# Last stage of a mixer: wo loaded through two queues, a gated tile in a free staging slot, transposes behind attention

## The chip, the cores and the metric

The kernel runs on one core of one Trainium2 chip. The metric is the device time of one execution in microseconds (us), the median of the runs; lower is better.

## What is computed

Two branches work on the same normalized input and are added to it. Branch A is linear attention with a softmax feature map, branch B a gated MLP whose gate mixes all 2048 tokens. All is float32.

```python
# S = 2048 tokens, D = 512, H = 32 heads of 16, Fh = 688
xn  = layernorm(x)
q, k, v = split_heads(xn @ wqkv)
phi(t)  = concat(softmax(t @ w_phi), softmax(-t @ w_phi))     # 32 features a head
kv  = phi(k)^T v ;  z = sum_s phi(k)
o   = phi(q) kv / (phi(q) z + 1e-6)
A   = o @ wo
zz  = gelu(xn @ w_in) ; z1 = zz[:, :Fh] ; z2 = layernorm(zz[:, Fh:])
B   = (z1 * (w_sp @ z2 + b_sp)) @ w_out
out = x + A + B
```

## The kernel before

The tokens lie in 16 tiles of 128 (`NT`), handled in pairs. A float32 product is made of three fp32r matmuls over a high part `h` and a rest `l` (`mm3`, lines L51 to L53): ScalarE rounds the high part (`round_h`, L43), VectorE subtracts to get the rest (`rest_l`, L47). The stages are: projections of the input and the sum `kv`; the second half of the MLP's input (`z2`, split into operands `B`); the token-mixing product in a seven-product block form (names P1 to P7, tile `g`); and the last stage, which this change touches.

In the seven-product stage a block of two row tiles takes four passes (`products`), `drain` adds the seven PSUM banks into `c` and `gate` multiplies by the gelu of `z1` and stores the gated tile to DRAM as `u_d`. The last block is drained when the last stage begins. Its passes also free the 16 slots of the pool `xz`, one after the other, as the operands `B` are used up; function `slot` gives such a slot to a tile of the last stage: six for `w_out` (`wu`), one each for `zb`, `u_uh`, `ul_rt`, `et`, `qtmp`, two for the first two feature tiles (`eq`), one for `et` of tile 3, one for `c`. One more slot comes free in the same pass and is not used until later.

The last stage computes, for each pair of tiles i and i+1:

- `attend_T`: 16 TensorE transposes of the features (`ptq`, L749 or L751), copied to `f` by ScalarE (L753); `attend`: the products with `kvT` (`po`, L765; sixteen in the program, which the profile counts as thirty-two), rounded and split into `oT` by ScalarE and VectorE.
- `gated`, that is `gate_T`: six transposes of a gated tile `u` (`ptu`, four on L640, then L644 and L645), split into `uh`, `ul` and `rt`.
- `project_u`: seventeen matmuls of `uh`, `ul`, `rt` with `wu` into `pout`; `project_o`: twelve matmuls of `oT` with `wo` into the same bank; then VectorE adds `x` (`xr`, L788) and SyncE stores the result.
- `features`: VectorE scales the features of a later tile (`q_fin`, L380 to L387), GpSimd's queue copies them to `er`.

Entering it, PE does in this order: the last `g` matmuls, the transposes of gated tile 1, `project_u(0)`, `attend_T(0)`, `project_u(1)`, `attend`, the transposes of gated tiles 2 and 3, `project_o(0)` and `project_o(1)`. The wo matrix is loaded in four chunks (`load_w`, `wof`), each by four transfers of 32 rows; ScalarE rounds a chunk to `woh`, VectorE makes `wol`.

A scheduler orders the instructions of each engine when the kernel is built; `tc.issue_after(ins)` only puts what stands inside it behind `ins` in that order. The waits come from the data and from reused memory. The queues are served in order: SyncE's (SP in the profile) carries nearly all loads of this stage, GpSimd's (POOL) the `er` copies and `z1t`. GpSimd's transfers are software queue q0 of the page, SyncE's are in hardware queue q1.

The lines that load wo and fetch gated tile 1:

```python
us[1] = fetch_u(1)                       # a tile of pool cw, opened when the last pass's memory is given back
...
load_w(wo, rows, wo_h[:, c], wo_l[:, c], cw.tile([P, D], F32, tag="wof", bufs=4, name="wof"))
```

Of the kernel before, what the change touches and what calls it, by code (L numbers as in the profile page):

```python
# [10 lines left out]
F32 = mybir.dt.float32  # L11
F32R = mybir.dt.float32r
# [6 lines left out]
P = 128  # L19
S, D, H, DH, FH = 2048, 512, 32, 16, 688  # L20
# [6 lines left out]
REM = FH - KF * P  # L27
# [8 lines left out]
def mixer(ctx: ExitStack, tc: tile.TileContext, x, x_t, wv, wqkT, phi_bd, wo, w_in, wst, b_r, w_out, out):  # L36
    nc = tc.nc
    pe, act, dve, pool, sp = nc.tensor, nc.scalar, nc.vector, nc.gpsimd, nc.sync


    def round_h(eng, h, src):
        if eng is act:
            return act.activation(h, src, AF.Copy).ins  # L43
        return eng.tensor_copy(h, src).ins

    def rest_l(l, src, h, eng=None):
        return (eng or dve).tensor_tensor(l, src, h.bitcast(F32), op=ALU.subtract).ins  # L47
# [113 lines left out]
    with ExitStack() as p0:  # L161
# [32 lines left out]
        def fold(wT, g, accs):  # L194
            gs = slice(g * P, (g + 1) * P)
            for c, acc in accs:
                ins = pe.matmul(acc[:, gs], wT[g][:, c * P:(c + 1) * P], bd[:, gs], start=g == 0, stop=g == NG - 1,
                                skip_group_check=True).ins
            return ins
# [26 lines left out]
        def split_x(src):  # L226
            t = xz.tile([P, 2, FH], F32R, tag="xz", name="xT")
            xT.append(t)
            src = src.rearrange("p a b -> p (a b)")
            return round_h(act, t[:, 0, :D], src), rest_l(t[:, 1, :D], src, t[:, 0, :D])  # L230

        def stats(s):
            st6 = wk.tile([P, 6], F32, tag="st6", name="st6")
            dve.bn_stats(st6, xt[s])
            nm = wk.tile([P, 1], F32, tag="nm", name="nm")
            ins = dve.bn_aggr(mv_x[:, s], st6).ins
            pool.tensor_scalar_mul(nm, mv_x[:, s, 0:1], -1.0)
            rstd_of(mv_x[:, s], r_x[:, s:s + 1])
            return nm, ins
# [4 lines left out]
        def transposed(s):  # L244
            xs = xt.pop(s)
            pt = ps.tile([P, ND, P], F32, tag="mm", name="pt")
            for c in range(ND):
                ins = pe.transpose(pt[:, c], xs[:, c * P:(c + 1) * P], ident).ins  # L248
            return pt, ins
# [46 lines left out]
        with ExitStack() as queue:  # L296
# [3 lines left out]
            nm, i = stats(0)  # L300
            keep(dve=i, act=center(0, nm))
            accs = [(c, (za, kv_ps_p)[c // 2].tile([P, D], F32, tag="z", name="fold")) for c in range(ND)]
            for g in range(NG):
                if g == NG - 1:
                    pt, i = transposed(0)
                    keep(pe=i)
                keep(pe=fold(wkT, g, accs))
            i, j = split_x(pt)
            keep(act=i, dve=j)
            nm, i = stats(1)  # L310
# [10 lines left out]
            pt, i = transposed(1)  # L321
            keep(pe=i)
            i, j = split_x(pt)
            keep(act=i, dve=j)
            nm, i = stats(2)
# [3 lines left out]
            for k in range(2):  # L329
                accs = [(2 * k + m, za.tile([P, D], F32, tag="z", name="fold")) for m in range(2)]  # L330
                for g in range(NG):
                    i = fold(wqT, g, accs)
                folded(0, accs)
                if k == 0:
                    keep(pe=i)
                    pt, i = transposed(2)
# [63 lines left out]
    def load_a(n):  # L400
        i, q = SEQ[n]
        f = []
        for k in range(2):
            t = ws.tile([P, QC, P], F32, tag=f"f{k}", bufs=2, name="wf")
            sp.dma_start(t, wst[2 * i + k, :, q * QC:(q + 1) * QC, :])
            f.append(t.rearrange("p (k two) t -> p two k t", two=2))
        return f
# [167 lines left out]
    def load_z1(i):  # L575
        t = gt.tile([P, 2, FH + REM], F32, tag="z1", name="z1t")
        for k in range(2):
            pool.dma_start(t[:, k, :FH], z1_d[2 * i + k])
        return t

    def products(n, g):
        i, q = SEQ[n]
        ops = A.pop(n)
        for name, an, bn in FORM:
            if n % NQ == 0:
                g[name] = psg.tile([P, D], F32, tag="g", name="g")
            dst = g[name][:, :FC]
            for k in range(2):
                (ah, al), (bh, bl) = ops[an], B[2 * q + k][bn]
                mm3(dst, (ah[:, k], al[:, k]), (bh, bl), n % NQ == 0 and k == 0, n % NQ == NQ - 1 and k == 1)  # L590
# [32 lines left out]
    def slot(name, dt=F32):  # L623
        return xz.tile([P, 2, FH], dt, tag="xz", name=name).rearrange("p a b -> p (a b)")

    def load_w(src, parts, h, l, t):
        rows = 0
        for r0, r1 in parts:
            sp.dma_start(t[rows:rows + r1 - r0], src[r0:r1, :])
            rows += r1 - r0  # L630
        return round_h(act, h, t[:rows]), rest_l(l, t[:rows], h)

    def load_u(i, t):
        sp.dma_start(t.bitcast(F32), u_d[i])
        return t
# [18 lines left out]
    def first_gate(i):  # L654
        a, b = slot("u_uh", F32R), slot("ul_rt", F32R)
        u = load_u(i, a[:, :FH + REM])
        return gate_T(psg, "g", u, k_tiles(a[:, FH + REM:]), k_tiles(b[:, :KF * P]), b[:2 * REM, KF * P:(KF + 1) * P])

    lasts, wu = [None] * 5, []

    def first_q(s):
        e = slot("eq", F32R)[:, :NF]
        sp.dma_start(e.bitcast(F32), e_d[s, :, :NF])
        return e

    def stage_w():
        t = [xz2.tile([P, 2, 2, FC], F32, tag="b", name="wof").rearrange("p a b c -> p (a b c)") for _ in range(3)]
        w = [slot("wu", F32R) for _ in range(KF + 1)]
        for c in range(KF + 1):
            n = P if c < KF else 2 * REM  # L670
            h, l = (w[c][:n, k * D:(k + 1) * D] for k in range(2))
            rows = [(c * P, (c + 1) * P)] if c < KF else [(KF * P, FH)] * 2
            load_w(w_out, rows, h, l, t[c // 2][:, c % 2 * D:(c % 2 + 1) * D])
            wu.append((h, l))

    g, es, ets = {}, {}, {}
    for n in range(NC):
        i = SEQ[n][0]
        if n % NQ == 1 and i < NP - 1:
            z = load_z1(i)  # L680
        products(n, g)
        if n % NQ == NQ - 1 and i < NP - 1:
            gate(i, drain(i, g, gt.tile([P, 4, FC], F32, tag="c", name="c")), z)
            g = {}
        if n + 3 < NC:
            raw[n + 3] = load_a(n + 3)
        if n + 2 < NC:
            A[n + 2] = prep_a(n + 2, raw.pop(n + 2))
        if n == NC - 4:
            stage_w()  # L690
        if n == NC - 3:
            zs = slot("zb", F32R)
            zb, ident_r = zs[:, :NF].bitcast(F32), zs[:, NF:NF + P]
            round_h(act, ident_r, ident)
            sp.dma_start(zb, zb_d)
            uT = [first_gate(0)]
            ets[2] = load_q(2, slot("et"))
            es[2], last = q_fin(ets.pop(2), slot("qtmp")[:, :NF], zb)
        if n == NC - 2:
            es[0], es[1] = first_q(0), first_q(1)  # L700
            ets[3] = load_q(3, slot("et"))
    cb = drain(NP - 1, g, slot("c").rearrange("p (a b) -> p a b", a=4))
# [4 lines left out]
    gt = p2.enter_context(right("gl", 1))  # L707
    cw = ctx.enter_context(left("cw", 1))
    wk = ctx.enter_context(left("cwk", 2))
    us, fin = {}, []  # L710

    def fetch_u(i):
        return load_u(i, cw.tile([P, FH + REM], F32R, tag="u", bufs=4, name="u"))
# [11 lines left out]
    def gated(z, ps=None):  # L725
        return gate_T(*(ps or (pst, "tr")), z, wk.tile([P, KF, P], F32R, tag="uh", name="uh"),
                      wk.tile([P, KF, P], F32R, tag="ul", name="ul"), wk.tile([2 * REM, P], F32R, tag="rt", name="rt"))

    us[1] = fetch_u(1)
    kvT = cw.tile([P, 2 * NG, QP], F32, name="kvT")  # L730
    with tc.issue_after(cb[1]), tc.issue_after(cb[2]):
        uT.append(gated(us.pop(1), (psg, "g")))
# [60 lines left out]
    wo_h, wo_l = (cw.tile([P, ND, D], F32R, name=f"wo{k}") for k in "hl")  # L793
    p = {0: project_u(0, uT.pop(0))}
    with tc.issue_after(lasts[0]), tc.issue_after(lasts[1]), tc.issue_after(fin[-1]):
        for c in range(ND):
            rows = [(r, r + QP) for r in range((c % 2 * NG * 2 + c // 2) * QP, D, 2 * QP)][:NG]
            load_w(wo, rows, wo_h[:, c], wo_l[:, c], cw.tile([P, D], F32, tag="wof", bufs=4, name="wof"))
    fT = attend_T(0)
    p[1] = project_u(1, uT.pop(0))  # L800
    oT, ins = attend(fT)
# [13 lines left out]
    nxt = {}  # L815
    for i in range(0, NT, 2):
        if i:
            p[i] = project_u(i, nxt.pop(i))
            if i + 2 < NT:
                nxt[i + 2] = gated(us.pop(i + 2))  # L820
            with tc.issue_after(lasts[2]):
                oT, _ = attend(fT)
            with tc.issue_after(lasts[3]):
                p[i + 1] = project_u(i + 1, nxt.pop(i + 1))
        else:
            nxt[2] = gated(us.pop(2))
        if i + 3 < NT:
            nxt[i + 3] = gated(us.pop(i + 3))
        for k in range(2):
            project_o(i + k, oT, p.pop(i + k))  # L830
            ahead(i + k)
        if i == GATE_LAST:
            with tc.issue_after(lasts[0]), tc.issue_after(lasts[1]):
                gate(NP - 1, cb, z)
            p2.close()
        if i + 2 < NT:
            with tc.issue_after(lasts[4]):
                fT = attend_T(i + 2)
# [33 lines left out]
```

## Time and profile before

| | us |
|---|---|
| runs | 648.68, 649.03, 650.23 |
| median of the runs | 649.03 |
| the profiled execution, its own time | 649.57 |
| its span in the profile | 647.8 |
| TensorE (PE) busy in it | 638.2 |
| VectorE (DVE) busy | 509.5 |
| ScalarE (ACT) busy | 278.7 |
| GpSimd (POOL) busy | 96.3 |

The span is the first to the last recorded instruction; the profiled execution took 1.8 us beside it. Times in rows of the trace count from the start of the span. The granted TensorE clock is full throughout (the page's row of tenths shows 9, which means 90% or more; the windows of the last stage show 1.00 or 0.99). Two of the three runs lie below the profiled execution.

A row of the timeline reads: start, duration, engine, line, operation, output and inputs, shape, count, and in brackets how long the engine sat idle before it and what ended that. Matmuls overlap in the pipeline, so the time that one takes away from the next is the distance of the starts, not the duration.

### The profile page before, as it was taken

Reading aid. Unit: us, or ns where it says so; the run is one execution under the profiler, and the core shown is the slowest. Engines: PE = TensorE matmul, PEld = TensorE weight load, DVE = VectorE, ACT = ScalarE, POOL = GpSimd, SP = SyncE. Lnnn points to the kernel's source line nnn. Section 1 sums busy time; section 2 is a strip of 40 time slices with the busy share of each in tenths; the row PEclk is TensorE's granted clock in tenths of the full one; section 3 lists DMA queues with packets and bytes.
Section 4 is the critical chain, followed back from the end, with each engine's and each line's share of the span. In section 5 each row is a group of like instructions: output and inputs, shape, how many; then the busy total and the mean of one; then the engine's idle time right before and its main releaser. Section 6 shows DMA issues by size and latency. Waiting matters only on the chain.

```text
span 647.8 us, 11206 instructions
## 1 busy us (share of the span) xinstructions
PE 638.2 (99%) x4291; PEld 576.1 (89%) x4291; DVE 509.5 (79%) x922; ACT 278.7 (43%) x464; POOL 96.3 (15%) x185
## 2 busy tenths in 40 slices
PE   7999999999999999999999999999999899999997
PEld 6888888888888999999999999999999677888885
DVE  4988888898889579889978778678696498989521
ACT  5644344332333437887443434434353332323330
POOL 3332221101100104542010010110100000001000
PEclk9999999999999999999999999999999999999999
DMA  8265345533463951002453352544548677775620
GB/s 308 76 165 129 110 119 121 155 114 102 125 183 98 291 187 66 2 2 65 142 179 124 122 175 79 172 128 120 178 157 277 201 271 261 243 264 222 225 66 32
DMA packets 39077, 98.12 MB, mean 151 GB/s; under 512 B 4880, under 2 KB 7184, under 8 KB 39024
## 3 DMA queue, kind: packets, MB, share of 16 engines
q1 hardware_dynamic: 27824, 56.51, 27.4%
q0 software_dynamic: 8896, 35.26, 18.0%
q10 hardware_dynamic: 2304, 5.64, 2.3%
q8 instruction: 33, 0.54, 0.3%
q14 instruction: 20, 0.16, 0.1%
HBM read 56.24 MB, written 26.48 MB: 128 GB/s over the span
## 4 chain that ended last, share of the span: by engine, by line
PE 95%; DMA 2%; DVE 1%; SPq 1%; ACT 0%; issue 0%; POOL 0%; ACTq 0%; POOLq 0%
PE g L53 11%; PE g L52 11%; PE g L51 11%; PE proj L53 7%; PE proj L51 7%; PE proj L52 7%; PE zps L53 6%; PE zps L52 6%; PE zps L51 6%; PE pout L51 5%; PE pout L53 5%; PE pout L52 5%; PE po L765 2%; PE kvps L273 1%; PE ptq L751 1%; PE pt L248 1%
## 5 line engine op out<-in xcount | busy, mean ns | idle before, releaser
L53 PE MATMUL g<-B,A 128*128 128x344 f32 x448 | 143.3, 320 | 0.0
L52 PE MATMUL g<-B,A 128*128 128x344 f32 x448 | 143.2, 320 | 0.0
L51 PE MATMUL g<-B,A 128*128 128x344 f32 x448 | 143.2, 320 | 0.0
L53 PEld LDWEIGHTS g<-B,A 128*128 128x128 f32 x448 | 84.2, 188 | 0.0
L51 PEld LDWEIGHTS g<-B,A 128*128 128x128 f32 x448 | 84.2, 188 | 0.0
L52 PEld LDWEIGHTS g<-B,A 128*128 128x128 f32 x448 | 84.1, 188 | 0.0
L47 DVE TENSOR_TENSOR A<-S,A 128x512 fp32r<-128x512 f32 x64 | 43.8, 690 | 33.6 <-ACT A L43 32.7
L43 ACT ACTIVATE A<-S 128x512 fp32r<-128x512 f32 x64 | 40.1, 631 | 58.9 <-PE g L53 36.0
L110 ACT ACTIVATE e<-e,r_x 128x1024 f32<-128x1024 f32 x32 | 36.8, 1151 | 41.2 <-DVE e L109 40.4
L51 PE MATMUL proj<-wqk_h,xT 128*128 128x512 f32 x128 | 51.4, 401 | 0.3 <-ACT wqk_h L43 0.3
L52 PE MATMUL proj<-wqk_l,xT 128*128 128x512 f32 x128 | 50.5, 394 | 1.1 <-DVE wqk_l L47 1.1
L43 ACT ACTIVATE A<-wf 128x512 fp32r<-128x512 f32 x64 | 33.4, 522 | 40.6 <-PE g L53 39.7
L53 PE MATMUL proj<-wqk_h,xT 128*128 128x512 f32 x128 | 50.9, 397 | 0.0
L51 PE MATMUL zps<-w_0h,xT 128*128 128x344 f32 x128 | 41.8, 326 | 0.0
L112 DVE TENSOR_REDUCE sm<-e 128x64 f32<-128x1024 f32 x32 | 38.7, 1208 | 3.3 <-ACT e L110 3.3
L51 PE MATMUL zps<-w_1h,xT 128*128 128x344 f32 x128 | 41.0, 320 | 0.0
L53 PE MATMUL zps<-w_0h,xT 128*128 128x344 f32 x128 | 41.0, 321 | 0.0
L53 PE MATMUL zps<-w_1h,xT 128*128 128x344 f32 x128 | 41.0, 320 | 0.0
L52 PE MATMUL zps<-w_0l,xT 128*128 128x344 f32 x128 | 40.9, 320 | 0.0
L52 PE MATMUL zps<-w_1l,xT 128*128 128x344 f32 x128 | 40.9, 319 | 0.0
L47 DVE TENSOR_TENSOR A<-wf,A 128x512 fp32r<-128x512 f32 x64 | 35.5, 555 | 3.4 <-ACT A L43 3.0
L753 ACT ACTIVATE f<-ptq 128x512 f32<-128x512 f32 x32 | 16.5, 602 | 33.6 <-PE ptq L751 27.1
(194 smaller groups left out, 1429.2 us busy)
## 6 DMA issues: line engine op xcount, KB each, us to landing
wf<-in_wst SPq DMA_DIRECT2D x64, 256.0 KB, 3.3
e_d<-e POOLq DMA_DIRECT2D x16, 544.0 KB, 5.0
et<-e_d SPq DMA_DIRECT2D x16, 544.0 KB, 5.2
zacc<-e POOLq DMA_DIRECT2D x16, 512.0 KB, 5.3
er<-et POOLq DMA_DIRECT2D x12, 512.0 KB, 4.1
u_d<-z1t POOLq DMA_DIRECT2D x16, 368.0 KB, 4.1
u<-u_d SPq DMA_DIRECT2D x15, 368.0 KB, 4.6
z_d<-z1f ACTq DMA_DIRECT2D x16, 344.0 KB, 3.4
```

Of the source, the lines that this page charges most:

```text
L43: return act.activation(h, src, AF.Copy).ins
L47: return (eng or dve).tensor_tensor(l, src, h.bitcast(F32), op=ALU.subtract).ins
L51: pe.matmul(dst, ah, bh, start=start, stop=False)
L52: pe.matmul(dst, ah, bl, start=False, stop=False)
L53: return pe.matmul(dst, al, bh, start=False, stop=stop).ins
L110: act.activation(e, e, AF.Exp, scale=scale)
L112: dve.tensor_reduce(sm, heads(e), axis=AX.X, op=ALU.add)
L248: ins = pe.transpose(pt[:, c], xs[:, c * P:(c + 1) * P], ident).ins
L273: pe.matmul(kv_acc[k:k + QP, m // 4], vs[:, m * QP:(m + 1) * QP], e[:, m * HP:(m + 1) * HP], start=s == 0 and m < 4, stop=s == NT - 1, ski ...
L751: pe.transpose(pt[:, a, k].bitcast(F32R), src, ident_r)
L753: act.activation(f, pt.rearrange("p a k b -> p a (k b)"), AF.Copy)
L765: lasts[3] = pe.matmul(po[r][c * QP:(c + 1) * QP, j // NG], kvT[rows, j], fs[j // 2][rows, j % 2], start=True, stop=True).ins
```

## The change

Three edits in the last stage. First, `load_w` gets the queue as an argument; wo's chunks 0 and 2 are loaded by SyncE, chunks 1 and 3 by GpSimd. Second, gated tile 1 is fetched into the free slot of `xz`, ahead of the loads of the first features, instead of into a tile of pool `cw`. Third, the transposes of the second gated tile of a pair come behind that pair's attention products in the order.

```diff
-    def load_w(src, parts, h, l, t):
+    def load_w(queue, src, parts, h, l, t):
         rows = 0
         for r0, r1 in parts:
-            sp.dma_start(t[rows:rows + r1 - r0], src[r0:r1, :])
+            queue.dma_start(t[rows:rows + r1 - r0], src[r0:r1, :])
...
-            load_w(w_out, rows, h, l, t[c // 2][:, c % 2 * D:(c % 2 + 1) * D])
+            load_w(sp, w_out, rows, h, l, t[c // 2][:, c % 2 * D:(c % 2 + 1) * D])
...
         if n == NC - 2:
+            us = {1: load_u(1, slot("u1", F32R)[:, :FH + REM])}
             es[0], es[1] = first_q(0), first_q(1)
...
-    us, fin = {}, []
+    fin = []
...
-    us[1] = fetch_u(1)
...
-            load_w(wo, rows, wo_h[:, c], wo_l[:, c], cw.tile([P, D], F32, tag="wof", bufs=4, name="wof"))
+            load_w((sp, pool)[c % 2], wo, rows, wo_h[:, c], wo_l[:, c], cw.tile([P, D], F32, tag="wof", bufs=4, name="wof"))
...
         if i + 3 < NT:
-            nxt[i + 3] = gated(us.pop(i + 3))
+            with tc.issue_after(lasts[3]):
+                nxt[i + 3] = gated(us.pop(i + 3))
```

The number of matmuls, of ScalarE and VectorE operations and of bytes moved stays the same. How the order changes is seen at three places.

On SyncE's queue, at the passage from the seven-product stage to the last one, the pieces of the two programs differ as follows (- before, + now; `u_5390` is gated tile 1 in its new slot, `eq` the first features, `wof` the rows of wo):

```order
 L634 DMA u_uh<-u_d 128x736
 L373 DMA et<-e_d 128x1088
+L634 DMA u_5390<-u_d 128x736
 L663 DMA eq<-e_d 128x1024 x2
 L373 DMA et<-e_d 128x1088
-L634 DMA u<-u_d 128x736
 L735 DMA kvT<-kvT_d 128x256
-L629 DMA wof<-in_wo 32x512 x16
+L629 DMA wof<-in_wo 32x512 x8
 L634 DMA u<-u_d 128x736 x2
```

Gated tile 1 moves ahead of three loads of features, which each come one place later, and eight of wo's sixteen transfers leave the queue.

On GpSimd's queue at the same passage:

```order
 L619 DMA u_d<-z1t 128x736 x2
 L578 DMA z1t<-z_d 128x688 x2
-L723 DMA er<-et 128x1024 x10
+L629 DMA wof<-in_wo 32x512 x8
+L724 DMA er<-et 128x1024 x10
 L619 DMA u_d<-z1t 128x736 x2
```

The eight transfers come behind the last load of `z1t` and ahead of all copies of features.

On ScalarE at the same passage (`c<-g` is the drain's first step, which copies P1's bank; `ptu_5332` is the second bank of gated tile 0's transposes):

```order
-L597 ACTIVATE c<-g 128x344
 L43 ACTIVATE u_uh<-ptu_5332 128x128
+L597 ACTIVATE c<-g 128x344
 L648 ACTIVATE ul_rt<-ptu_5332 96x128
 L43 ACTIVATE uh<-ptu 128x512
 L43 ACTIVATE uh<-ptu_5475 128x128
 L648 ACTIVATE rt<-ptu_5475 96x128
-L43 ACTIVATE woh<-wof 128x512 x4
-L753 ACTIVATE f<-ptq 128x512 x4
+L43 ACTIVATE woh<-wof 128x512 x3
+L753 ACTIVATE f<-ptq 128x512 x4
+L43 ACTIVATE woh<-wof 128x512
```

The drain's first step now stands behind a rounding of gated tile 0, and the last chunk of wo behind the four copies to `f`.

On PE, in the pair i = 2 of the last stage, before (the block left out is the rest of `project_u`):

```order
L645 MATMUL ptu_5760<-zb,u 96x128
L765 MATMUL po<-f,kvT 32x256 x12
L640 MATMUL ptu<-zb,u 128x128 x4
L765 MATMUL po<-f,kvT 32x256 x4
L51 MATMUL pout<-wu,uh 128x512
...
L779 MATMUL pout<-wu,rt 128x512 x2
L644 MATMUL ptu_5818<-zb,u 128x128
L645 MATMUL ptu_5818<-zb,u 96x128
```

and now:

```order
L645 MATMUL ptu_5760<-zb,u 96x128
L765 MATMUL po<-f,kvT 32x256 x16
L51 MATMUL pout<-wu,uh 128x512
...
L779 MATMUL pout<-wu,rt 128x512 x2
L640 MATMUL ptu<-zb,u 128x128 x4
L644 MATMUL ptu_5818<-zb,u 128x128
L645 MATMUL ptu_5818<-zb,u 96x128
```

The four transposes that cut the attention products of pair i = 2 in two now stand behind `project_u`; in pair i = 4 the same is moved, and from pair 6 on PE's order is as it was, since there the transposes already stood behind.

## The prediction

> **What bounds the kernel now.** I read the page first, then PE's list of waits, then PE's timeline through the last stage, and last the timelines of the engines and queues that PE waits for there.
>
> ```profile
> PE 638.2 (99%) x4291; PEld 576.1 (89%) x4291; DVE 509.5 (79%) x922; ACT 278.7 (43%) x464; POOL 96.3 (15%) x185
> ...
> PE 95%; DMA 2%; DVE 1%; SPq 1%; ACT 0%; issue 0%; POOL 0%; ACTq 0%; POOLq 0%
> ```
>
> PE is busy nearly always, and 95% of the chain that ended last is PE's own work. So time is saved only where PE waits, or where its order costs extra. The list of PE's waits from 480 us on has two lines (total, times, longest):
>
> ```profile
> PE ptu L640 <- DMA u<-u_d: 1.3, 1, 1.3
> PE po L765 <- ACT f L753: 0.7, 1, 0.7
> ```
>
> Both are where the last stage begins. PE's timeline there, one row for each change of work:
>
> ```profile
> 503.08 0.32 PE L53 MATMUL g<-B,A 128*128 128x344 f32 x1
> 504.75 0.52 PE L640 MATMUL ptu<-zb,u 128*128 128x128 f32 x4 [1.35 <-DMA u<-u_d]
> ...
> 505.25 0.47 PE L51 MATMUL pout<-wu,u_uh 128*128 128x512 f32 x1
> ...
> 509.26 1.49 PE L751 MATMUL ptq<-zb,eq 128*128 128x128 f32 x16
> ...
> 514.14 0.62 PE L779 MATMUL pout<-wu,rt 96*128 96x512 f32 x2
> 515.50 2.10 PE L765 MATMUL po<-f,kvT 64*32 64x256 f32 x32 [0.74 <-ACT f L753]
> 517.53 0.53 PE L640 MATMUL ptu<-zb,u 128*128 128x128 f32 x4
> ...
> 518.54 0.46 PE L51 MATMUL pout<-woh,oT 128*128 128x512 f32 x1
> ```
>
> The last `g` matmul starts at 503.08, the first transpose of gated tile 1 at 504.75: 1.67 us. Then `po` starts late and takes 2.03 us (515.50 to 517.53).
>
> **First edit costed: gated tile 1 in the free slot.** SyncE's queue and the time that such a load needs (issue to landing; least, median, most):
>
> ```profile
> 490.59 3.63 SPq L663 DMA_DIRECT2D eq<-e_d  x2
> ...
> 497.65 0.32 SPq L634 DMA_DIRECT2D u<-u_d  x1
> ...
> 503.33 7.75 SPq L629 DMA_DIRECT2D wof<-in_wo  x16
> ```
>
> ```profile
> DMA to landing us min/median/max: 3.0/4.6/7.2
> ```
>
> Before, the load goes out at 497.65, because its tile reuses memory that the last pass still reads, and lands when PE has been waiting for a while. Now it takes the place and the slot of the first `eq`, so it goes out at 490.59 and lands at 497.8 even with the longest landing, 5 us ahead of use. The features that move back one place are used at 509.26 at the earliest, over 10 us after their new places, and hide their delay there. So PE's 1.67 us shrink to the distance of matmuls back to back, 0.16 (the `g` rows follow each other so; half their 0.32): **1.51 us**, unless another wait takes over. The candidate is the drain: ScalarE's first step of it now stands behind a rounding, and `project_u(0)` needs a bank that VectorE's fourth step (L601) frees. ScalarE's rows, then VectorE's first and last of the seven from drain step one to four:
>
> ```profile
> 497.61 0.46 ACT L597 ACTIVATE c<-g 128x344 f32<-128x344 f32 x1 [2.01 <-PE g L53]
> 499.78 0.28 ACT L43 ACTIVATE u_uh<-ptu 128x128 fp32r<-128x128 f32 x1 [1.71 <-PE ptu L645]
> ...
> 514.33 0.63 ACT L43 ACTIVATE woh<-wof 128x512 fp32r<-128x512 f32 x1 [3.25 <-DMA wof<-in_wo]
> 514.87 2.04 ACT L753 ACTIVATE f<-ptq 128x512 f32<-128x512 f32 x4
> ...
> 529.02 2.06 ACT L753 ACTIVATE f<-ptq 128x512 f32<-128x512 f32 x4 [6.41 <-PE ptq L749]
> ```
>
> ```profile
> 498.63 0.58 DVE L596 SCALAR_TENSOR_TENSOR c<-g,bias,c 128x344 f32<-128x344 f32 x1
> ...
> 501.55 0.52 DVE L601 TENSOR_TENSOR c<-g,c 128x344 f32<-128x344 f32 x1 [0.32 <-PE g L53]
> ```
>
> The copy now ends at 499.78 + 0.28 + 0.46 = 500.52 instead of 498.07. From the first VectorE step to the end of the fourth it took 3.44 us before, with waits for PE in it; at worst it takes that again and ends at 503.96. PE reaches `project_u(0)` at 503.24 + 0.50 = 503.74. So the loss is at most 0.2 us, and I take none, since the products it waited for are then long there.
>
> **Second edit costed: wo through two queues.** The four copies to `f` stand behind the roundings of all wo chunks on ScalarE, and the last rounding began at 514.33, after idling 3.25 us for its rows. SyncE needed 7.75 us for the sixteen issues (0.48 each), which is most of the way from 503.33 to 514.33. Now SyncE issues eight and GpSimd eight, and only three chunks stand ahead of `f`. No row shows a 32-row transfer from GpSimd's queue. The nearest are these (count | busy, mean ns) and the landing of `er`:
>
> ```profile
> L270 POOL DMA_DIRECT2D zacc<-e x16 | 14.6, 911 | 92.4 <-DVE e L269 64.4 <-ACT z1f L139 10.9 <-DVE e L113 9.2
> ...
> L723 POOL DMA_DIRECT2D er<-et x12 | 6.4, 530 | 96.5 <-DVE et L387 83.0 <-PE ptu L645 7.2 <-issue 6.3
> ```
>
> ```profile
> er<-et POOLq DMA_DIRECT2D x12, 512.0 KB, 4.1
> ```
>
> I take 0.53 us for an issue, as of the plain copy; the accumulating one at 0.91 is the upper bound, SyncE's 0.48 the lower. GpSimd waits for P3's matmuls, whose bank VectorE reads just after step four, about 502.5. Chunk 1 is then issued by 504.6 and landed by 508.7, chunk 3 by 506.7 and 510.8. ScalarE rounds chunk 1 by 509.4 and has `f` done 2.04 later, 511.4. PE comes to `po` at 503.24 + (514.14 + 0.47 - 504.75) = 513.10. So the wait is gone, with 1.7 us to spare, and so is the slow run of `po`, which went at the pace of the copies. The price of `po` with `f` ready is in pair 6:
>
> ```profile
> 565.92 1.09 PE L765 MATMUL po<-f,kvT 64*32 64x256 f32 x32
> 566.95 0.50 PE L51 MATMUL pout<-wu,uh 128*128 128x512 f32 x1
> ...
> 570.53 0.64 PE L779 MATMUL pout<-wu,rt 96*128 96x512 f32 x2
> 571.00 0.46 PE L640 MATMUL ptu<-zb,u 128*128 128x128 f32 x4
> ...
> 571.46 0.47 PE L51 MATMUL pout<-woh,oT 128*128 128x512 f32 x1
> ```
>
> `po` takes 1.03, the two `rt` matmuls 0.47. So 514.14 to 517.53, 3.39 us, becomes 1.50: 1.89. If transposes after `po` cost what they seem to cost in pair 2 (below: 0.99 for 24 of the 32), `po` takes up to 1.25 and the gain is 1.67. I take **1.8 us**. Chunk 3 has a later deadline: its rest on VectorE stands ahead of the split of `oT`, wanted at 518.54 - 3.4 = 515.1. It is rounded and split by 510.8 + 1.3 = 512.1, or just behind the copies at 513. The loads queued behind wo on SyncE (gated tiles, `x`) go out some 3.7 us earlier and only gain; the `er` copies behind it on GpSimd begin near 529, long after.
>
> A rule of the Trainium skill speaks against this edit: "DMA: Bandwidth & Descriptors", section "Issuing engines are not separate DMA queues", says that all issuing engines feed the same 16 DMA engines and that spreading saves only the time to initiate, usually small. Here 7.75 us of initiating are on the path, so the trace bears the exception out; by the rule this term would be near zero and the time 646.3, the second rival below.
>
> **Third edit costed: transposes behind attention.** Pair 2 before, and two rows of pair 4:
>
> ```profile
> 530.44 1.07 PE L765 MATMUL po<-f,kvT 64*32 64x256 f32 x24
> 531.43 0.54 PE L640 MATMUL ptu<-zb,u 128*128 128x128 f32 x4
> 531.90 0.64 PE L765 MATMUL po<-f,kvT 64*32 64x256 f32 x8
> 532.47 0.50 PE L51 MATMUL pout<-wu,uh 128*128 128x512 f32 x1
> ...
> 536.53 0.23 PE L644 MATMUL ptu<-zb,u 128*128 128x128 f32 x1
> 536.59 0.22 PE L645 MATMUL ptu<-zb,u 128*96 128x128 f32 x1
> 536.65 0.45 PE L51 MATMUL pout<-woh,oT 128*128 128x512 f32 x1
> ...
> 548.30 1.07 PE L765 MATMUL po<-f,kvT 64*32 64x256 f32 x24
> ...
> 550.33 0.50 PE L51 MATMUL pout<-wu,uh 128*128 128x512 f32 x1
> ```
>
> `po` with the four transposes inside takes 2.03 (530.44 to 532.47, and again 548.30 to 550.33) and the two others 0.12. In pair 6, where all six stand behind `project_u`, it is 1.03 + 0.46. The difference is 2.15 - 1.49 = 0.66; twice, for pairs 2 and 4: **1.32 us**. The eight last `po` must not now wait for `f`: the fourth copy ends at 529.02 + 2.06 = 531.08, 0.64 after `po`'s start, and they are due at three quarters of 1.03, 0.77. That is a margin of 0.13.
>
> **The sum.** 1.51 + 1.8 + 1.32 = 4.6 us off PE's path, with nothing behind it that I find late. The profiled execution, 649.57, becomes 644.9. It was 0.54 above the median of the runs, 649.03, which becomes 644.4. I say 644.5.
>
> **The rivals.** *GpSimd's issues are slow here* (ends slower). Chunk 3 must be through by 515.1, so with t for an issue 502.5 + 8t + 4.1 + 1.3 may not pass it: t = 0.9. Each 0.1 more costs 0.8 us, and at t = 0.9 + 4.6/8 = 1.5 the whole gain is gone. At 2 us it is 644.5 + 8 x 1.1 = 653.3. For it: no such transfer in the trace. Against it: all rows lie at 0.53 to 0.91, the plain ones while VectorE works at full load. The Trainium skill's "SBUF — State Buffer", section "SBUF: two separate sides", names a way: a VectorE operation in a two-port mode keeps GpSimd from writing descriptors, with 3.1 us quoted for a transfer that takes 0.62 alone; an estimate by that page is 644.5 + 8 x 2.2 = 662. The `er` row's 530 ns speaks against it.
>
> *wo is held by the transfer, not by the issue.* Then the second term is missing: 646.3. For it: the last of the sixteen was issued by 511.08 and ScalarE started at 514.33, 3.2 us of landing that no queue saves. Against it: this landing now begins 3.7 us earlier.
>
> *The third term is eaten*, by the wait for `f` or by VectorE:
>
> ```profile
> 518.54:536.65 18.11, 18.11 (x121) 14.31 (x120) 17.24 (x29) 6.74 (x17) 0.53 (x1) 1.00 0.75 261
> ```
>
> From one `project_o` to the next VectorE is busy 17.24 of 18.11 us (fifth figure), so a PE 0.66 quicker leaves it 0.2. If it becomes the bound, 1.32 is missing: 645.8.
>
> *The first wait is only replaced*, by the drain or a late landing: 1.5 missing, 646.0. Were the first two terms both missing, it is 647.8, no change.
>
> **How the numbers follow.** All three terms: 0.62, 644.5, itself between 643.7 and 645.3. One missing: wo's 0.09, the transposes' 0.08, the first's 0.06. Two or more missing, or a new wait of some 3 us: 0.10, 647 to 650. Slow issues on GpSimd: 0.05. By the runs shown 0.3% (1.9 us) is about what a measurement can tell from no change, so faster means below 647.1: 0.84; same 0.11; slower 0.05. The range 643.7 to 647.1 takes in every case with one term missing and leaves the last two and a little below.
>
> **What would show it.** Right: no wait of PE for `u`; `ptu` 0.16 to 0.2 after the last `g`; `po` of the first pair at 1.0 to 1.3 us, without a wait for `f`; pairs 2 and 4 at 1.03 for an unbroken `po`; GpSimd's eight issues at 0.5 to 0.6 each; the last stage's later pairs as long as before. Wrong: ScalarE idle for `wof` late, a `pout` that waits for VectorE's drain, or pairs whose length is VectorE's.

## The result, and the profile after

The changed kernel took 645.91 us (median of four runs, 645.63 to 646.0), the kernel before beside it 649.11 (four runs, 648.68 to 650.23): a ratio of 0.9945, with a 95% interval of 0.9932 to 0.9957. The forecast was 644.5, within 643.7 to 647.1. So the sign and the range held, and the gain was 3.2 us where 4.5 was said. The profiled execution after took 645.63, its span is 643.8.

PE's list of waits from 480 us on is empty now; both lines of before are gone. This is PE's timeline of the changed kernel at the same places (start, duration, engine, line, operation, shape, count):

```profile
503.33 0.32 PE L53 MATMUL g<-B,A 128*128 128x344 f32 x1
503.49 0.46 PE L640 MATMUL ptu<-zb,u 128*128 128x128 f32 x4
...
503.94 0.46 PE L51 MATMUL pout<-wu,u_uh 128*128 128x512 f32 x1
...
513.36 1.09 PE L765 MATMUL po<-f,kvT 64*32 64x256 f32 x32
514.39 0.54 PE L640 MATMUL ptu<-zb,u 128*128 128x128 f32 x4
...
515.42 0.47 PE L51 MATMUL pout<-woh,oT 128*128 128x512 f32 x1
...
527.30 1.34 PE L765 MATMUL po<-f,kvT 64*32 64x256 f32 x32
528.57 0.50 PE L51 MATMUL pout<-wu,uh 128*128 128x512 f32 x1
...
532.61 0.46 PE L640 MATMUL ptu<-zb,u 128*128 128x128 f32 x4
...
533.06 0.47 PE L51 MATMUL pout<-woh,oT 128*128 128x512 f32 x1
...
550.53 0.46 PE L51 MATMUL pout<-woh,oT 128*128 128x512 f32 x1
```

From the last `g` to the first `woh` product it is 515.42 - 503.33 = 12.09 us, before 518.54 - 503.08 = 15.46: 3.37 less. The next pair takes 17.64 instead of 18.11, the one after it 17.47 instead of 17.87 (before, its `woh` product began at 554.52). Together that is 4.24 us less in the last stage. The stage itself began 0.25 later in this execution (503.33 against 503.08), so the span is 4.0 shorter. A second profiled execution of the changed kernel, 646.41 us, shows the same 12.09 us at the entry (504.01 to 516.10).

SyncE, GpSimd and ScalarE of the changed kernel at the entry:

```profile
490.85 0.32 SPq L634 DMA_DIRECT2D u<-u_d  x1
...
497.90 0.32 SPq L735 DMA_DIRECT2D kvT<-kvT_d  x1
501.33 3.77 SPq L629 DMA_DIRECT2D wof<-in_wo  x8
```

```profile
502.53 3.94 POOL L629 DMA_DIRECT2D wof<-in_wo  x8 [4.28 <-PE g L53]
```

```profile
506.89 0.62 ACT L43 ACTIVATE woh<-wof 128x512 fp32r<-128x512 f32 x1
507.74 1.15 ACT L43 ACTIVATE woh<-wof 128x512 fp32r<-128x512 f32 x2 [0.23 <-DMA wof<-in_wo]
508.80 2.04 ACT L753 ACTIVATE f<-ptq 128x512 f32<-128x512 f32 x4
511.47 0.63 ACT L43 ACTIVATE woh<-wof 128x512 fp32r<-128x512 f32 x1 [0.63 <-DMA wof<-in_wo]
```

GpSimd's eight issues take 0.49 us each. `f` is done at 510.84, and PE comes to `po` at 513.36, so 2.5 us are in hand. One thing was not in the prediction: `kvT` goes out at 497.90 instead of 502.96, and wo's rows start at 501.33 instead of 503.33. With gated tile 1's tile gone from pool `cw`, the tiles behind it lie in memory that the last passes give back earlier: SyncE's issue of `kvT` waited 4.9 us for PE's `g` before and waits 1.6 now.

### The profile page after: what moved, and what is told of

It reads as the page before. It is cut to its first block, busy times and chain, and to the rows that moved or that the text cites. A ratio compares the mean times of both kernels' runs of the same rounds, so it can differ in the third digit from the quotient of the medians.

```text
span 643.8 us, 11202 instructions
## 1 busy us (share of the span) xinstructions
PE 635.9 (99%) x4291; PEld 575.6 (89%) x4291; DVE 508.5 (79%) x922; ACT 278.4 (43%) x464; POOL 100.3 (16%) x193
## 4 chain that ended last, share of the span: by engine, by line
PE 97%; DMA 1%; DVE 1%; ACT 0%; SPq 0%; issue 0%; POOL 0%; POOLq 0%
PE g L53 11%; PE g L52 11%; PE g L51 11%; PE proj L53 7%; PE proj L51 7%; PE proj L52 7%; PE zps L53 6%; PE zps L51 6%; PE zps L52 6%; PE pout L51 6%; PE pout L53 5%; PE pout L52 5%; PE kvps L273 1%; PE ptq L751 1%; PE po L765 1%; PE pt L248 1%
## 5 line engine op out<-in xcount | busy, mean ns | idle before, releaser
L51 PE MATMUL pout<-wu,uh 128*128 128x512 f32 x75 | 30.8, 410 | 0.0
```

Source lines behind the costliest of these rows:

```text
L51: pe.matmul(dst, ah, bh, start=start, stop=False)
```

## The experiments

Medians in us with the number of runs; the kernel before was run beside each. The ratio is worked out over the runs and need not be that of the medians.

| kernel | median (runs) | before | ratio, 95% interval |
|---|---|---|---|
| free slot alone | 647.74 (6) | 649.47 | 0.9972, 0.9961 to 0.9984 |
| two queues alone | 650.49 (11) | 649.47 | 1.0007, 0.9995 to 1.0019 |
| transposes alone | 648.94 (11) | 649.47 | 0.9987, 0.9979 to 0.9996 |
| slot and transposes | 646.16 (7) | 649.47 | 0.9959, 0.9943 to 0.9975 |
| the same, again | 646.44 (12) | 649.26 | 0.9961, 0.9950 to 0.9973 |
| the change, again | 646.06 (6) | 649.26 | 0.9946, 0.9935 to 0.9958 |
| two queues, GpSimd's later | 647.84 (6) | 649.85 | 0.9965, 0.9951 to 0.9978 |
| gated tile 1 late | 652.66 (4) | 649.26 | 1.0044, 1.0030 to 1.0059 |
| wo all on GpSimd | 648.91 (10) | 649.85 | 0.9984, 0.9973 to 0.9994 |
| GpSimd's chunks in 8 rows | 659.19 (4) | 649.85 | 1.0142, 1.0123 to 1.0161 |
| a chunk in one transfer | 654.91 (6) | 649.26 | 1.0080, 1.0068 to 1.0093 |
| `project_u` before attention | 647.23 (5) | 649.85 | 0.9961, 0.9945 to 0.9977 |

**The free slot alone.** Against the kernel before:

```diff
+            us = {1: load_u(1, slot("u1", F32R)[:, :FH + REM])}
             es[0], es[1] = first_q(0), first_q(1)
-    us[1] = fetch_u(1)
```

> The free slot for gated tile 1 alone; wo's sixteen transfers all stay on SyncE. Theory: PE's 1.67 us between the last g and the first transpose of gated tile 1 become 0.16, and since kvT and wo's rows then lie in memory that is given back earlier, wo's issues start about 2 us earlier on SyncE too, so the wait for f does not grow: 1.5 to 2.0 us faster than before. Rival: wo's rows still pace f, PE comes to po 1.5 us earlier and waits 1.5 us longer there (2.2 instead of 0.7): no faster.

1.73 us faster by the medians. The profiled execution, one of the two quickest of the six (646.65 to 648.77), shows no wait of PE, though all sixteen issues are SyncE's:

```profile
498.41 0.32 SPq L735 DMA_DIRECT2D kvT<-kvT_d  x1
501.84 7.71 SPq L629 DMA_DIRECT2D wof<-in_wo  x16
```

```profile
503.84 0.32 PE L53 MATMUL g<-B,A 128*128 128x344 f32 x1
...
515.93 0.47 PE L51 MATMUL pout<-woh,oT 128*128 128x512 f32 x1
```

That is 12.09 us again, the changed kernel's own figure. So in this execution the slot alone removed both waits, because wo's issues begin 2.00 us ahead of the last `g` here, and 0.25 behind it before. The rival, that PE would only wait longer for `f`, falls for this execution. The other four runs took 0.6 to 1.9 us longer and have no profile, so the slot does not show this full gain every time; what SyncE's queue does in some executions is seen further down.

**The two queues alone, and the same with GpSimd's transfers later.** Against the kernel before, and the second against the first:

```diff
-            load_w(wo, rows, ...)
+            load_w((sp, pool)[c % 2], wo, rows, ...)
```

```diff
-    sp.dma_start(kvT.rearrange("p j b -> p (j b)"), kvT_d)
+    for queue, half in ((sp, slice(0, 64)), (pool, slice(64, P))):
+        queue.dma_start(kvT.rearrange("p j b -> p (j b)")[half], kvT_d[half])
```

> Two queues for wo alone; gated tile 1 stays in its tile of pool cw. Theory: PE's wait for u stays at 1.3 us; the wait for f goes, and po of the first pair runs in 1.0 to 1.3 us instead of 2.0: 1.7 to 1.9 us faster than before. Rival (wo is held by the transfer, not by the issue): f comes as late as before, less than 0.5 us faster.

> The two queues alone, as in the kernel that took 650.49, but with kvT loaded in two halves, one by each queue, so that GpSimd's transfers of wo's rows begin behind the last use of kvT's memory, near 503.5, and not at 498.9 beside the load of gated tile 1. Theory (those early transfers delay gated tile 1, PE's wait grows to 1.8 us, and TensorE's granted clock then falls to half for 3.4 us): the wait for u is 1.4 us or less as before the change, the mean clock is 0.999 or more in nearly all executions, and the time is 1.5 to 1.9 us less than before. Rival (the fallen clock has nothing to do with those transfers): about half of the executions show a clock below 0.998 again, and the median is no less than before.

The first gave no gain, against my theory. These are, from its profiled execution, PE's one wait, a row of GpSimd's queue, and windows of PE (the window, its length, PE's busy time, then the granted clock, the share of the DMA engines and GB/s):

```profile
PE ptu L640 <- DMA u<-u_d: 1.8, 1, 1.8
```

```profile
498.87 1.98 POOL L629 DMA_DIRECT2D wof<-in_wo  x4
```

```profile
506.00:508.00 2.00, 1.93 (x12) 0.92 0.69 195
508.00:510.00 2.00, 2.00 (x6) 0.50 0.62 166
510.00:512.00 2.00, 2.00 (x8) 0.73 0.87 312
512.00:514.00 2.00, 2.00 (x20) 1.00 0.90 289
```

The wait for `f` is gone as said. But PE waited 1.79 us for gated tile 1's load, which landed 7.4 us after its issue at 498.54, and GpSimd's first four transfers ran beside it from 498.87. Then the granted clock stood at 0.50 for about 3.4 us: by the windows, 0.08 x 2 + 0.50 x 2 + 0.27 x 2 = 1.70 us of full-rate time lost, as much as the edit gained. Of the eleven runs, the four with a mean clock of 0.999 or more took 648.39 to 648.78, the seven with 0.994 to 0.997 took 649.94 to 652.92.

With GpSimd's transfers of wo held until 504.7 the wait was 0.90, all six runs had a clock of 0.999 or more, and the median was 2.0 below before's. From last `g` to first `woh` it took 13.23 us (504.00 to 517.23). So the second edit is worth about 2 us by itself (1.4 to 3.2 by the ratio's interval), if the clock does not fall with it. That GpSimd's early transfers bring the fallen clock is borne out by counting runs: seven of eleven with them, none of the 25 of the kernel before that were run beside them, and none of the six with the transfers later. That they do so by delaying gated tile 1's load is not shown: the load took 7.4 us with them, but also 7.0 in the profile before, 6.5 with them held back, and 5.9 in that of the transposes alone.

**Gated tile 1 late.** Against the kernel before: its load behind `kvT`'s.

```diff
-    us[1] = fetch_u(1)
+    u1 = cw.tile([P, FH + REM], F32R, tag="u", bufs=4, name="u")
     kvT = cw.tile([P, 2 * NG, QP], F32, name="kvT")
+    sp.dma_start(kvT.rearrange("p j b -> p (j b)"), kvT_d)
+    us[1] = load_u(1, u1)
```

> The kernel before, with gated tile 1's load put behind kvT's on SyncE, so that it goes out near 503.3 and not at 497.7: PE's wait for it grows from 1.3 to 4 to 6 us. Behind it the wait for f and the slow po (1.9 us) vanish, since wo has that much more time. Theory (a wait of this length also costs TensorE's clock half of its rate for 3.4 us, 1.7 us of work): 3 to 5 us slower than before, and a stretch of the granted clock at 0.50 behind the wait in all executions. Rival (only the wait counts): 1 to 3 us slower, the clock at 1.00.

3.4 us slower. The wait was 3.94 us, the wait for `f` had gone, and all four runs showed a mean clock of 0.993 to 0.997:

```profile
507.29 0.72 PE L640 MATMUL ptu<-zb,u 128*128 128x128 f32 x4 [3.94 <-DMA u<-u_d]
```

```profile
505.50:506.00 0.50, 0.00 (x0) 0.78 0.91 309
...
512.50:513.00 0.50, 0.50 (x4) 0.90 0.77 206
```

The clock fell during the wait, near 505.8, and came back near 512.6: 6.8 us in this execution, twice the 3.4. About 1.5 us of the stretch lay in the wait itself and cost nothing; the other 5.3 us, from 507.29 on, cost half of their length, some 2.6 us. The theory holds in kind, and the stretch was longer than it said.

**The transposes alone.** Against the kernel before:

```diff
+            with tc.issue_after(lasts[3]):
+                nxt[i + 3] = gated(us.pop(i + 3))
-            nxt[i + 3] = gated(us.pop(i + 3))
```

> The transposes behind attention alone. By the changed kernel's trace po takes 1.27 us in pairs 2 and 4 and the six transposes behind it 0.45, 1.72 instead of 2.15: 0.43 us less for each pair, 0.87 us faster than before. By the prediction's own term (po at 1.03, margin kept) it would be 1.32 us faster. Rival: the pair's length is VectorE's, starts of project_o stay 18.1 us apart: no faster.

The profile shows 17.63 and 17.43 us between the starts of `project_o` (before 18.11 and 17.87), 0.92 less. The medians differ by 0.53 and the ratio's interval reaches from 0.3 to 1.4 us, so the time alone would not tell 0.87 from 1.32; the rows do. The rival, VectorE's pace, falls.

**`project_u` before attention,** in pairs 2 and 4 of the changed kernel, so that `f` is 4 us old when `po` begins:

```diff
+                with tc.issue_after(lasts[2]):
+                    p[i + 1] = project_u(i + 1, nxt.pop(i + 1))
+                with tc.issue_after(lasts[5]):
+                    oT, _ = attend(fT)
```

> The changed kernel with the attention products of pairs 2 and 4 behind project_u of the second tile, 4 us after the copies to f. Theory (po's 1.27 us there are a hidden wait for the fourth f): po takes 1.03 in both pairs. What it gives back: project_o then comes 0.45 us behind po, where the first half of oT is rounded only 0.7 us behind po, so a wait of about 0.3 us takes the place of the 0.24: as fast as the changed kernel within 0.3 us. Rival (the 1.27 are not f's doing): po still takes 1.27 there, and the time is 0.5 us longer than the changed kernel's.

```profile
532.09 1.09 PE L765 MATMUL po<-f,kvT 64*32 64x256 f32 x32
533.11 0.54 PE L640 MATMUL ptu<-zb,u 128*128 128x128 f32 x4
...
549.46 1.09 PE L765 MATMUL po<-f,kvT 64*32 64x256 f32 x32
550.48 0.54 PE L640 MATMUL ptu<-zb,u 128*128 128x128 f32 x4
```

`po` takes 1.02 in both, against 1.27 and 1.26 after the change. So those 0.25 were a wait for `f` that no list named. They come back behind `po`: the two pairs take 17.72 and 17.37, together 35.09, against 17.64 and 17.47, 35.11. It is no improvement: by the medians it is 2.6 us faster than before where the change gives 3.2, more than the expected 0.3 apart but within the intervals. A later pair took 17.65 instead of 16.92; there `po` came out cut into 24 and 8 around a `project_u`.

**Slot and transposes without the queues, and the change again beside it.** Against the changed kernel, wo back on SyncE:

```diff
-            load_w((sp, pool)[c % 2], wo, rows, ...)
+            load_w(wo, rows, ...)
```

> The change without the two queues: wo all on SyncE, the free slot and the transposes behind attention kept. If wo's start on SyncE moves 2 us earlier by the slot alone, f comes some 2 us earlier against 1.5 for PE, so a wait for f of up to 0.5 us and a slow po stay: 2.4 to 3.1 us faster than before, and 0.9 to 1.6 us slower than the changed kernel. Rival 1: the slot alone relieves wo, the queues then bring nothing: as fast as the changed kernel within 0.4 us. Rival 2: wo still paces f wholly: only 0.9 us faster than before.

> The change without the two queues once more, beside the changed kernel on the same chip. Theory (SyncE's sixteen issues are in time unless the queue halts for 2 us): two groups of executions, one at the changed kernel's time within 0.5 us, one 2 to 3 us above it, the second in a third to a half of them. Rival: one group, in time always or late always.

> The changed kernel once more. Theory (eight issues leave it 2.5 us in hand at po): one group of executions, none 1.5 us or more above the median, 3 to 4 us faster than before. Rival: it falls into the same two groups as with wo all on SyncE.

By the medians the queues add 0.25 us (646.16 against 645.91, which were not measured side by side) and 0.4 (646.44 against 646.06, side by side). Neither is clear of the noise. By the ratios, which count every run, it is 0.9 to 1.0 us. So my first expectation of 0.9 to 1.6 us missed by the median, where its first rival fits, and the difference lies in a tail. Of nineteen runs without the queues eight took over 647.3, up to 649.71; of ten with them none was over 647.0. The eight are spread from 647.38 to 649.71 and do not form the second group, 2 to 3 us up, that I expected. The profile of one such execution (648.92) shows where its time went:

```profile
PE po L765 <- ACT f L753: 1.7, 1, 1.7
```

```profile
501.68 11.00 SPq L629 DMA_DIRECT2D wof<-in_wo  x16
```

```profile
SPq L629 <- DMA kvT<-kvT_d: 1.9, 1, 1.9
```

SyncE's sixteen issues took 11.00 us, not 7.7. For 1.9 us an issue waited for `kvT`, the load eight places ahead of it on this queue, to land. The profile of the second round (647.45) shows the same halt, 1.3 us long, sixteen issues in 9.01 us and a wait of PE for `f` of 0.66. In the first of the two a second halt names no wait: the last issue alone lasted 2.18 us (1.83 in the execution of the transposes alone), while the DMA engines were idle:

```profile
511.00:512.00 1.00, 1.00 0.27 78
512.00:513.00 1.00, 1.00 0.05 8
```

Its cause was not found, and the other six of the eight have no profile.

**wo all on GpSimd, and GpSimd's chunks in transfers of 8 rows.** Against the changed kernel:

```diff
-            load_w((sp, pool)[c % 2], wo, rows, ...)
+            load_w(pool, wo, rows, ...)
```

```diff
+            if c % 2:
+                rows = [(r, r + 8) for r0, r1 in rows for r in range(r0, r1, 8)]
             load_w((sp, pool)[c % 2], wo, rows, ...)
```

> The changed kernel with all four chunks of wo through GpSimd's queue, sixteen issues. Theory (an issue there takes 0.5 us whatever else runs): the issues run from 502.5 to 510.5, the last chunk is rounded by about 515.5 and just in time for project_o: less than 0.6 us slower than the changed kernel, that is 2.6 to 3.6 us faster than before. Rival (GpSimd's issues are slow beside VectorE's work): at 0.9 us and more for an issue they end at 517 or later, and project_o waits 2 us or more.

> The changed kernel with chunks 1 and 3 cut into transfers of 8 rows, thirty-two issues on GpSimd instead of eight, the same bytes. Theory (the price is one per issue, 0.5 us, whatever the rows): they run from 502.5 to 518.5, the last chunk lands near 522, and project_o, wanted at 515.4, waits some 5 to 7 us: 2 to 4 us slower than before. Rival (the price goes by rows): 4 us for all of them as now, no slower than the changed kernel.

The first lost 2.3 us of the change's 3.2, the second is 9.3 us slower than before. Both are worse than the theory, and not by the price of an issue, which stayed at 0.5 us for 32 rows and for 8. This is GpSimd's timeline, and its waits for wo, of the first:

```profile
502.24 3.45 POOL L629 DMA_DIRECT2D wof<-in_wo  x7 [3.35 <-PE g L53]
506.42 1.53 POOL L629 DMA_DIRECT2D wof<-in_wo  x3 [0.73 <-DMA z1t<-z_d]
508.87 0.50 POOL L629 DMA_DIRECT2D wof<-in_wo  x1 [0.93 <-DMA wof<-in_wo]
```

```profile
POOL wof L629 <- DMA wof<-in_wo: 3.4, 5, 1.0
```

Seven go out without a halt. The eighth waits for `z1t`, eight places ahead on this queue, to land, and later ones wait for wo's own. By these waits, and SyncE's for `kvT`, a queue of this program has at most eight transfers in flight. The landing took 6.4 us (median), so the queue's pace became one in 0.8 on average, and the last issue went out at 513.94 instead of 502.24 + 15 x 0.5 = 509.7. ScalarE's rounding of the third chunk then stood ahead of the rounding of `oT`, and `project_o` waited:

```profile
518.19 0.50 PE L51 MATMUL pout<-woh,oT 128*128 128x512 f32 x1 [1.30 <-ACT oT L43]
```

With thirty-two issues the last went out near 525 and PE waited for wo's operands, 6.3 us at the longest, with the clock at 0.50 from 524.9 to 535.1.

The change puts only eight issues of wo on each queue, so they can be held by the loads ahead of them, but not by each other. That happens: with the two queues alone GpSimd's eighth waited 1.65 us for `z1t`, and with the transfers of 8 rows SyncE's eighth waited 2.1 us for `kvT`. In both profiles of the changed kernel no issue waited so; there `kvT` landed 0.2 to 0.3 us before SyncE's eighth went out.

**A chunk in one transfer.** Slot and transposes, wo on SyncE in four transfers instead of sixteen:

```diff
-            load_w(wo, rows, ...)
+            src = wo.rearrange("(a g b r) n -> a b g r n", a=2, b=2, r=QP)[c % 2, c // 2]
+            sp.dma_start(t, src)
```

> The change with the free slot and the transposes behind attention, and wo all on SyncE, each chunk of four times 32 rows in one transfer: four issues instead of sixteen, the same bytes. Theory (the issues were the price, not the queue that makes them): the issues end near 504 instead of 509, f is through before PE comes to po, and no wait is left: as fast as the changed kernel within 0.5 us, without GpSimd. Rival (the bytes, or the landing, are the price): f comes as late as with the sixteen, 1 to 3 us slower than the changed kernel.

It is 5.7 us slower than before, so theory and rival both missed. The four issues were over at 506.08, but the rows came late:

```profile
506.00:507.00 1.00, 1.00 0.27 104
507.00:508.00 1.00, 1.00 0.26 100
```

```profile
PE po L765 <- ACT f L753: 6.2, 1, 6.2
```

While the first of them ran, the share of the DMA engines stood at a quarter, four of sixteen, and ScalarE got a chunk every 3.1 to 4.3 us. The Trainium skill's "DMA: Bandwidth & Descriptors", section "Rules for kernel authors", says that the slowest dimension of the pattern with more than one element sets how many engines a transfer uses. Here that is 4, and the share of 0.26 agrees. PE's wait of 6.2 us also brought the clock down to 0.50, from 518.2 to 525.0 in this profile, and all six runs had a mean clock of 0.992 to 0.995, so a part of the 5.7 us is the clock's.

## Why the prediction was right or wrong

**First edit, 1.51 us: right for the execution it was read from.** From the last `g` to the first `ptu` it is 0.16. The drain is not late: PE goes from `ptu` to `project_u(0)` without a wait, which was taken as nothing and is nothing.

**Second edit, 1.8 us: right in size, and only half right in what brings it.** From the `rt` matmuls (512.82) to `ptu` (514.39) it takes 1.57 instead of 3.39, so 1.82. The step that failed is that SyncE's start on wo was taken as fixed at 503.33. It hung on the memory that `kvT` and wo's rows get, and the first edit moved it 2 us ahead. With that, SyncE alone can be in time (12.09 in the slot's own profile), and the queues add 0.25 to 0.4 us in the median and the end of the tail. Without the slot, the queues are worth about 2.0 us while the clock holds, so the two gains overlap rather than add. The sum came out because each wait was counted once; that the wait was charged to the queues and mostly removed by the slot did not show in it, which is luck.

The prediction's 1.7 us to spare were not sure either. They follow GpSimd's chunk 1 alone, while SyncE's chunk 2 stands ahead of `f` too. By the prediction's own rows its issues end at 503.33 + 8 x 0.48 = 507.2. With the 1.8 to 3.5 us that wo's rows took to land before, the rounding (0.63) and the copies (2.04), `f` is done between 511.7 and 513.4, and PE was to come at 513.10. The earlier start made this harmless.

The Trainium skill's "DMA: Bandwidth & Descriptors", section "Issuing engines are not separate DMA queues", which calls the saving usually small, was said to have an exception here. The runs give both: about 2.0 us where the issues were on the path, 0.25 to 0.4 in the median where the slot had taken them off it.

**Third edit, 1.32 us: the mis-sized term, 0.87.** Pairs 2 and 4 have `po` at 1.27 and 1.26 and transposes at 0.45 behind it, 1.72 and 1.71 instead of 2.15. The step that failed is that the eight last `po` "are due at three quarters of 1.03, 0.77" behind the start. This divided the time by the count, but `po`'s 1.03 holds a tail behind the last issue. In the kernel with `project_u` before attention, where `f` is ready, the weights of the last eight (`po`'s own loads on PEld) begin to load 0.46 behind `po`'s start, so that is when the eight are due. The fourth copy to `f` ends 0.66 behind `po`'s start:

```profile
525.89 2.07 ACT L753 ACTIVATE f<-ptq 128x512 f32<-128x512 f32 x4 [6.38 <-PE ptq L749]
```

525.89 + 2.07 = 527.96, against 527.30. The last eight weights begin to load at 528.00, 0.70 behind the start. So the margin of 0.13 was a wait of about 0.24. With `f` ready early, `po` took 1.02.

**The sum.** 1.51 + 1.82 + 0.87 is 4.2 us in the last stage, where 4.6 was said. The rest of the miss lies in the executions: the stage began 0.25 later in after's profiled one, which was 0.28 below its median, and before's was 0.46 above its own. The first wait is not the same in all: 1.35 in before's profile, 0.32 in that of the transposes alone, whose load is the same. There the wait for `f` is 1.27 instead of 0.74, and the entry takes 15.00 us instead of 15.46. A sum made against one execution takes its waits at that execution's size.

**The rivals.** Slow issues on GpSimd: 0.49 us, so no. wo held by the transfer: no, by the two queues alone with GpSimd's later. VectorE as the bound of pairs 2 and 4: no, PE waits for it nowhere on its list, though it is busy 17.21 (fifth figure) of pair 2's 17.64 us and so has little to spare:

```profile
515.42:533.06 17.64, 17.64 (x121) 14.24 (x120) 17.21 (x29) 6.17 (x16) 0.57 (x1) 1.00 0.71 248
```

The wait for `f` did eat a third of the third term, as that rival's other half said, but not all of it.

## What to carry to other kernels

Before summing the edits of a change, ask what each does to the start of the others: a tile that leaves a pool moves the memory, and so the start, of all that is allotted behind it. A wait hidden in a run of pipelined matmuls shows only as the run's length, so compare it with the same run elsewhere (1.27 against 1.03) and don't divide its duration by its count to say when its last part is due. Two waits in a row on one engine are one budget (1.35 and 0.74 in one execution, 0.32 and 1.27 in another); removing the first pays in full only if the second's producer also comes earlier.

## What was not expected of the hardware

A wait of PE can cost more than its length. After 1.79 us of waiting the granted clock stood at 0.50 for 3.4 us and 1.7 us were lost; with 3.94 us of waiting it stood there for 6.8, with 6.2 (a chunk in one transfer) for 6.8, and with 6.3 (transfers of 8 rows, a wait of 2.7 soon behind it) for 10.2. With 1.35 and 1.69 us (the profiles of before, and of slot and transposes) it stayed at 1.00. The length of the wait is not all that decides: two of the sixty runs of the kernel before that were run beside the experiments, and one of eleven of the transposes alone, also had a mean clock of 0.996 to 0.997. What else decides stays open. The Trainium skill's "TensorE: Matmul & The Clock Gate", section "Part 1: The HAM clock gate", gives a free-running window of about 3.4 us. The low stretches agree with it, being one, two and three such lengths; that an idle window of that length is needed does not, as 1.79 us were enough in this trace.

An issue on GpSimd's queue took 0.50 us whether it moved 32 rows or 8. On both queues a transfer waited for the one eight places ahead of it to land, where that one had not landed yet.
